# Batch 0 as one block of 512 columns and eight blocks behind it, batches 0 and 1 by a written list of steps, weights converted 1024 columns at a time

## The chip, the cores and the metric

The kernel runs on one core of a Trainium2 chip. The metric is the device time of one launch in microseconds (us). TensorE (PE, and PEld for its weight loads), VectorE (DVE), ScalarE (ACT), GpSimd (POOL) and SyncE (SP, which issues all the DMAs here) run their own instruction streams, each in order.

## The reference

Attention within chunks of 64 positions, then an MLP mixer over tokens and channels. There are 8 batches, 8 heads, 576 positions and 64 features per head; DT is 256 and DC is 1536.

```python
scores = scale * np.matmul(q_c, k_c.transpose(0, 1, 2, 4, 3))     # per chunk of 64
scores = scores - np.max(scores, axis=-1, keepdims=True)
attn = np.exp(scores); attn = attn / (np.sum(attn, axis=-1, keepdims=True) + 1e-09)
out = np.matmul(attn, v_c)                                         # x: [8, 576, 512]
h = np.maximum(xt @ w_tok1, 0.0) @ w_tok2                          # xt: x transposed
u = x + h.transpose(0, 2, 1)
return u + np.maximum(u @ w_ch1, 0.0) @ w_ch2                      # 512 -> 1536 -> 512
```

The four weights are 64-bit floats in memory, all else is 32-bit.

## The kernel before

**Columns.** The mixer works on u with features on partitions and (batch, position) pairs as columns: 8 x 576 = 4608 columns. Batch 0 is done first, as two halves of 288 columns (`HALF`). Then come the other 4032 columns as `BLOCKS`: six of 512 and two of 480. The first two (`SINGLE`) run one by one. The other six run as three pairs in `pair` and `pair_end`, by a scheme that forms seven products for the eight of two blocks (`ps_p`, from weight sums stored in DRAM and read back through a `ring`).

**One block.** For each of the twelve slices f of the 1536 hidden features, `ch1` forms 12 matmuls into `ps_c` (four groups of input features, and three terms, `THREE`, since each operand is split into a high and a low part), ScalarE takes the ReLU as `gh`, VectorE the remainder as `gl`, and `ch2` adds 12 matmuls into the four accumulators `acc`. So a block that isn't in a pair costs 288 matmuls of its width; a pair costs 252 for `ps_p` and 288 for `acc`.

**Batch 0.** The loop over f forms `ch1` for the first half, `ch1` for the second half, whose ReLU is parked in `g1` (`kept=True`), and `ch2` for the first half. A second loop then splits the parked values (`split_g`) and does `ch2` for the second half. The token mixing of batch 0 (`tok1_first`, `tok2`) runs in plain fp32; `tok2` adds x by transposing matmuls. The second half's `tok2` stands behind the first `ch1`.

**Weights.** `plan` lists 29 pieces: five of the token weights, and 24 of 512 columns in turn from w_ch1 (`c1`) and w_ch2 (`c2`). Each takes four steps on ScalarE (`wtop`, `low` and its second half in `words_clamp`, `kept` in `split_high`) and four on VectorE (clamp, shift, add, `split_low`). `conversion()` is a generator; `convert(n)` places its next n VectorE steps, by counts in tables (`FIRST_FILL`, `END_FILL`, `STEP_FILL`). The token weights are converted at the start, and their parts for later batches are split in the second loop of batch 0 (`SPLIT_AT`).

**Attention.** There are 36 tiles, nine for two batches; the fifth of the nine is shared by both. A tile is: scores (32 matmuls of 64 columns), row maximum, subtraction, exp, transposition, values (32 matmuls), division. The five tiles of batch 0 transpose on TensorE (`near`). Those of batch 1 (`part`, placed by `STARTS`) transpose in 32 x 32 blocks on VectorE and finish through DRAM: `far` is written, and read back as `pf`. Tiles of batches 2 to 7 run in "bursts" (`attention`, `LAG` 2: the values of a tile stand two bursts behind its scores). The first two bursts stand in the second loop of batch 0 (`FIRST_QK`), fourteen in the two single blocks (`BURSTS`, a place being one `ch1` or one `ch2`), the others in the pairs.

**What sets the order.** Up to the first `start_ps.close()` the source's order holds on TensorE, ScalarE and VectorE. Between there and `HAND_FROM` a list scheduler orders them; from there on TensorE is again in the source's order (`by_hand`), and `in_turn` holds single steps behind the last one. SP is in the source's order throughout.

Of the kernel before, what the change touches and what calls it, by code (L numbers as in the profile page):

```python
# [18 lines left out]
P = 128  # L19
# [10 lines left out]
HALF = S // 2  # L30
# [19 lines left out]
BURSTS = (2, 6, 9, 13, 17, 20, 23, 26, 30, 34, 37, 38, 40, 43)  # L50
# [3 lines left out]
TOKENS_AT = (19, 35, 44)  # L54
# [5 lines left out]
KEPT_AT = {18 + k: ((k // 3, (0, 1, 5)[k % 3]),) for k in range(18)}  # L60
# [7 lines left out]
AHEAD = 3  # L68
RUN = 4

WARM_T = (0, 1, 0, 0, 0)
WARM_V = (0, 0, 1, 0, 0)
FIRST_FILL = (2, 2, 2, 3, 1)
PREPARE = (0, 1, 2, 1, 1)

END_FILL = (3, 2, 2, 3, 6, 1, 1)
STEP_FILL = (2, 4, 4, 4, 4, 4, 4, 2, 0, 2, 5, 3, 0, 8, 5, 4, 4, 5, 7, 4, 1, 1, 5, 3)

STARTS = ((9, 10, 10, 10, 14), (13, 14, 15, 16, 16), (17, 18, 18, 19, 22), (23, 23, 24, 26, 27))
# [26 lines left out]
def attention_mixer_kernel(ctx, tc, qk_in, vo_in, v_in, w1_in, w2_in, wc1_in, wc2_in, out):  # L108
# [68 lines left out]
    fetched = []  # L177

    def fetch(n):
        for i in range(len(fetched), min(n, len(plan))):  # L180
            fetched.append(i)
            key, src, lo, n = plan[i]
            nc.sync.dma_start(
                out=raws[i][1].rearrange("p n w -> p (n w)"), in_=src[:, lo:lo + n].bitcast(I32)
            )

    def words_scalar(i):

        fetch(i + AHEAD)
        n = plan[i][3]
        st = raws[i][1]
        if i < token:
            if "t" not in tops:
                tops["t"] = pool.tile([P, sum(p[3] for p in plan[:token])], F32, tag="wtt", name="wtt", bufs=1)
            lo = sum(p[3] for p in plan[:i])  # L200
            tops[i] = tops["t"][:, lo:lo + n]
        else:
            tops[i] = pool.tile([P, n], F32, tag="wt", name="wtop", bufs=4)
        lows[i] = pool.tile([P, max(n, DM)], I32, tag="low" if n < S else "low_t", name="low", bufs=3)[:, :n]
        nc.scalar.activation(out=tops[i], in_=st[:, :, 1].bitcast(F32), func=AF.Copy, scale=REBIAS)  # L205
        nc.scalar.activation(  # L206
            out=lows[i].bitcast(I16)[:, 0::2], in_=st[:, :, 0].bitcast(U32), func=AF.Copy, scale=2.0 ** -29
# [3 lines left out]
    def words_clamp(i):  # L211
        nc.vector.tensor_scalar(
            out=tops[i], in0=tops[i], scalar1=-MOST, scalar2=MOST, op0=ALU.max, op1=ALU.min
        )
        nc.scalar.copy(out=lows[i].bitcast(F16)[:, 1::2], in_=tops[i])
# [43 lines left out]

    def split_high(i):  # L260
# [1094 lines left out]
```

## Time and profile before

| | us |
|---|---|
| median of three runs (lowest, highest) | 741.07 (738.27, 741.98) |
| the profiled execution, its own time | 743.39 |
| the profiled execution, its span | 741.4 |
| TensorE busy, 5730 matmuls | 717.3 |
| VectorE, ScalarE, GpSimd busy | 437.1, 275.4, 189.6 |

The span runs from the first instruction to the last one. Matmuls overlap, so busy time of TensorE is no measure of how close it comes to its rate; the number of matmuls in a stretch is. "Idle before" names what ended the wait of an engine.

### The profile page before, as it was taken

The numbers are of one execution on the slowest core, as the hardware profiler recorded it, in microseconds if no ns is written. First come the engines' busy times: TensorE is split into PE (matmuls) and PEld (weight loads), VectorE is DVE, ScalarE is ACT, GpSimd is POOL, SyncE is SP. The second block draws the span as 40 slices with busy tenths as digits, with TensorE's granted clock in tenths as the row PEclk, the third lists the DMA queues.
The fourth block names the chain that finished last, engine by engine and source line by source line (L and its number), as shares of the span: only waits on it lengthen the run. The fifth ranks groups of instructions, "written<-read, shape, count | busy, mean of one in ns | idle before, by whom it ended". The sixth has DMA issues, their size and how long they took to land.

```text
span 741.4 us, 14629 instructions
## 1 busy us (share of the span) xinstructions
PE 717.3 (97%) x5730; PEld 629.7 (85%) x5730; DVE 437.1 (59%) x735; ACT 275.4 (37%) x505; POOL 189.6 (26%) x161
## 2 busy tenths in 40 slices
PE   6899998999999999989999999999999999999997
PEld 4488898988889877878888888988888899999997
DVE  4799966555546546577666763686343539433361
ACT  5899953333332333332333333332211324112120
POOL 0000012162346543103111163061112602311220
PEclk8999999999999999999999999999999999999999
DMA  9956346669855676745888995045655430644111
GB/s 344 407 218 222 118 157 198 218 202 290 289 178 185 202 229 224 237 127 197 268 261 272 284 312 139 12 140 161 192 177 182 138 93 21 235 135 126 53 54 53
DMA packets 93268, 139.94 MB, mean 189 GB/s; under 512 B 10832, under 2 KB 44880, under 8 KB 93200
## 3 DMA queue, kind: packets, MB, share of 16 engines
q1 hardware_dynamic: 93200, 139.02, 57.0%
q8 instruction: 45, 0.74, 0.4%
q14 instruction: 23, 0.19, 0.1%
HBM read 98.34 MB, written 39.71 MB: 186 GB/s over the span
## 4 chain that ended last, share of the span: by engine, by line
PE 74%; DMA 8%; DVE 6%; ACT 5%; SPq 4%; issue 2%; POOL 0%; DVEq 0%; ACTq 0%; POOLq 0%
PE acc L1121 24%; PE ps_p L1051 21%; PE acc L726 8%; PE ps_c L682 7%; PE ps_t L653 5%; PE ps_t L581 4%; SPq L406 2%; DMA far<-blocks 2%; PE ps_sv L372 2%; PE ps_sv L384 1%; DMA raw_t<-in_w 1%; DVE wtop L225 1%; ACT low L206 1%; PE sum L590 1%; ACT wtop L205 1%
## 5 line engine op out<-in xcount | busy, mean ns | idle before, releaser
L1121 PE MATMUL acc<-gh,kept_c 128*128 128x512 f32 (+1 forms) x576 | 169.5, 376 | 0.0
L1051 PE MATMUL ps_p<-bh,ring 128*128 128x512 f32 (+1 forms) x504 | 148.5, 376 | 0.1
L1121 PEld LDWEIGHTS acc<-gh,kept_c 128*128 128x128 f32 x576 | 108.2, 189 | 12.8
L1121 PE MATMUL acc<-gl,kept_c 128*128 128x512 f32 (+1 forms) x288 | 107.9, 375 | 0.0
L1051 PEld LDWEIGHTS ps_p<-bh,ring 128*128 128x128 f32 x504 | 94.6, 189 | 11.8 <-DVE sum L1146 0.5
L1051 PE MATMUL ps_p<-bl,ring 128*128 128x512 f32 (+1 forms) x252 | 94.4, 375 | 0.0
L726 PE MATMUL acc<-gh,kept_c 128*128 128x288 f32 (+1 forms) x384 | 91.1, 341 | 1.7 <-ACT gh L695 1.5
L484 POOL TENSOR_TENSOR xl<-x,xh 128x512 fp32r<-128x512 f32 x28 | 37.7, 1358 | 160.4 <-ACT xh L483 137.2
L726 PEld LDWEIGHTS acc<-gh,kept_c 128*128 128x128 f32 x384 | 63.7, 192 | 8.2 <-ACT gh L695 2.8
L1148 POOL TENSOR_TENSOR sum<-snap,sum 128x512 f32<-128x512 f32 (+1 forms) x18 | 23.1, 1282 | 167.4 <-ACT snap L1140 144.7
L1121 PEld LDWEIGHTS acc<-gl,kept_c 128*128 128x128 f32 x288 | 54.4, 189 | 6.5
L682 PE MATMUL ps_c<-uh,kept_c 128*128 128x512 f32 x192 | 57.8, 383 | 1.3 <-DVE rl L600 1.3
L726 PE MATMUL acc<-gl,kept_c 128*128 128x288 f32 (+1 forms) x192 | 57.1, 336 | 0.0
L1051 PEld LDWEIGHTS ps_p<-bl,ring 128*128 128x128 f32 x252 | 47.6, 189 | 5.7
L1153 ACT ACTIVATE gh<-c 128x512 fp32r<-128x512 f32 (+1 forms) x36 | 22.4, 622 | 77.3 <-DVE c L1146 73.4
L352 ACT ACTIVATE pr<-pr 128x512 f32<-128x512 f32 x36 | 22.6, 628 | 76.6 <-DVE pr L348 76.6
L1140 ACT COPY snap<-ps_p 128x512 f32<-128x512 f32 (+1 forms) x36 | 20.8, 577 | 75.5 <-PE ps_p L1051 71.9
L1154 DVE SCALAR_TENSOR_TENSOR gl<-g,gh 128x512 fp32r<-128x512 f32 (+1 forms) x36 | 32.9, 936 | 24.4 <-ACT gh L1153 24.4
L696 DVE SCALAR_TENSOR_TENSOR gl<-ps_c,gh 128x512 fp32r<-128x512 f32 (+1 forms) x36 | 21.8, 605 | 40.1 <-ACT gh L695 40.0
L682 PE MATMUL ps_c<-both,kept_c 128*128 128x288 f32 x288 | 41.2, 291 | 1.0 <-DVE gl L696 1.0
L682 PEld LDWEIGHTS ps_c<-uh,kept_c 128*128 128x128 f32 x192 | 35.7, 189 | 6.8 <-DVE rl L600 1.7
L682 PEld LDWEIGHTS ps_c<-both,kept_c 128*128 128x128 f32 x288 | 37.2, 189 | 2.2 <-DVE gl L696 1.4
(134 smaller groups left out, 1257.8 us busy)
## 6 DMA issues: line engine op xcount, KB each, us to landing
ring<-w SPq DMA_DIRECT2D x126, 256.0 KB, 4.0
qk<-in_qk SPq DMA_DIRECT2D x36, 512.0 KB, 4.8
far<-blocks SPq DMA_DIRECT2D x63, 256.0 KB, 2.9
raw_c<-in_wc SPq DMA_DIRECT2D x24, 512.0 KB, 9.3
pf<-far SPq DMA_DIRECT2D x124, 64.0 KB, 2.4
v<-in_v SPq DMA_DIRECT2D x27, 256.0 KB, 4.6
xt<-far SPq DMA_DIRECT2D x96, 64.0 KB, 2.0
w<-sparts SPq DMA_DIRECT2D x24, 256.0 KB, 2.7
```

Of the source, the lines that this page charges most:

```text
L352: nc.scalar.activation(out=pr, in_=pr, func=AF.Exp, scale=1.0 / float(D) ** 0.5)
L484: nc.gpsimd.tensor_tensor(out=xl, in0=t["own"], in1=xh.bitcast(F32), op=ALU.subtract)
L581: nc.tensor.matmul(ps, lhsT=lhsT, rhs=in_turn_of_two(rhs), start=(n == 0 and q == 0), stop=(n == len(mt) - 1 and q == len(terms) - 1),)
L653: nc.tensor.matmul(ps[:, at:at + n], lhsT=lhsT[:, cols], rhs=rhs.rearrange("p (c a b) -> p c b a", a=2, b=RUN), start=(q == 0), stop=(q == ...
L682: nc.tensor.matmul(ps[:, :width], lhsT=weights["c1", f][:, wi, k // 2, k % 2 * P:(k % 2 + 1) * P], rhs=in_turn_of_two(u[ui][k]), start=(k ...
L696: nc.vector.scalar_tensor_tensor(out=halved(gl), in0=ps, scalar=0.0, in1=halved(gh.bitcast(F32)), op0=ALU.max, op1=ALU.subtract)
L726: nc.tensor.matmul(accs[e], lhsT=weights["c2", f][:, wi, e * P:(e + 1) * P], rhs=in_turn_of_two(g[gi]), start=(f == 0 and q == 0), stop=(f ...
L1051: nc.tensor.matmul(ps, lhsT=w[:, wi, j * P:(j + 1) * P].bitcast(F32R), rhs=in_turn_of_two(u[ui][j]), start=j == 0 and q == 0, stop=j == 1 ...
L1121: nc.tensor.matmul(accs[e], lhsT=weights["c2", f][:, wi, e * P:(e + 1) * P], rhs=in_turn_of_two(g[gi]), start=start and q == 0, stop=stop ...
L1148: engine.tensor_tensor(out=c, in0=a, in1=b, op=ALU.add)
L1153: nc.scalar.activation(out=gh, in_=c, func=AF.Relu)
L1154: nc.vector.scalar_tensor_tensor(out=gl, in0=c, scalar=0.0, in1=gh.bitcast(F32), op0=ALU.max, op1=ALU.subtract)
```

## The change

Batch 0 becomes one block of its first 512 columns; the 64 that are left (`REST`) go into the next block, beside 448 of batch 1, so that all eight `BLOCKS` are 512 wide. The parking in `g1`, `split_g` and the last blocks of 480 go away. `u` of a block is one tile for each part. Of the 64 columns, `more` does the token mixing, and `moreh`, `morel` put them into block 0.

`plan` has 15 pieces: two of w_tok1, one of w_tok2, and twelve of 1024 columns (two f each). Its steps are no longer placed by a generator: the string `ORDER` names every step of batches 0 and 1, from the first load to the end of batch 0's `ch2`, and TensorE, ScalarE, VectorE and SP all take it in that order. `F` fetches a piece, `top low clamp sign shift add high rest` are its eight steps; `s max sub exp` and `t` or `far`, then `pt v za zb o end split` those of an attention tile; `u uh ul` the token mixing of batch 0; `ca gh gl cb` a slice's `ch1`, its two parts and its `ch2`; `hidden rh rl turn` batch 1's token mixing; `D` stores weights. The shared fifth tile of batches 0 and 1 is stacked in `stack`. Of batch 1's tiles the last transposes on TensorE (`t8`). The parts of the token weights are split earlier (`high0`, `high1`, `high2`). All sixteen first bursts stand in the single blocks.

```diff
-HALF = S // 2
+REST = S - 512
-BLOCKS = [(k * N, N) for k in range(2 * PAIRS)]
-LAST = ((B - 1) * S - 2 * PAIRS * N) // 2
-BLOCKS += [(2 * PAIRS * N + k * LAST, LAST) for k in range(2)]
+BLOCKS = [((k + 1) * N, N) for k in range(SINGLE + 2 * PAIRS)]
-BURSTS = (2, 6, 9, 13, 17, 20, 23, 26, 30, 34, 37, 38, 40, 43)
+BURSTS = (0, 3, 6, 9, 12, 15, 18, 21, 24, 27, 30, 33, 36, 38, 40, 43)
-TOKENS_AT = (19, 35, 44)
+TOKENS_AT = (21, 36, 44)
...
+ORDER = """
+LQ0 F0 LV0 LQ1 LV1 LQ2 F1 LV2 LQ3 LV3 LQ4 LV4 F2 F3 F4 F5 F6 F7 LQ5 LV5 F8 LQ6 LV6 F9 F10 s0 max0 top0
+sub0 low0 clamp0 exp0 sign0 s1 t0 shift0 max1 pt0 add0 s2 sub1 high0 max2 exp1 v0 rest0 top1 t1 za0 sub2
...
+low6 ul1 s5 clamp6 uh3 max5 low7 ul3 sub5 ca0 sign6 rest4 exp5 end4 top7 shift6 ca1 far5 gh0 clamp7 high5
+F11 LQ7 LV7 gl0 sign7 add6 cb0 gh1 rest5 high6 shift7 stack0 ca2 gl1 top8 add7 low8 clamp8 ca3 rest6
...
+rest2 gh7 pt7 morel0 gl7 v7 add14 LV9 cb7 D5 za7 high14 zb7 o7 rest14 split7 s8 LQ10 gh9 end7 cb8 max8
+gl9 sub8 ca10 exp8 gh10 gl10 t8 pt8 cb9 v8 LV10 za8 zb8 o8 ca11 split8 end8 gh11 gl11
+hidden0 rh0 rl0 hidden1 rh1 rl1 cb10 turn0 cb11
+"""
...
-    plan = [(("t1", j, min(2, NKT - j)), w1_in, j * DT, min(2, NKT - j) * DT) for j in range(0, NKT, 2)]
-    plan += [(("t2", k), w2_in, k * S, S) for k in range(NT1)]
+    plan = [(("t1", 0, 2), w1_in, 0, 2 * DT), (("t1", 2, 3), w1_in, 2 * DT, 3 * DT)]
+    plan += [(("t2", 0, NT1), w2_in, 0, NT1 * S)]
     token = len(plan)
-    for f in range(-1, NFC):
-        plan += [(("c1", f + 1), wc1_in, (f + 1) * DM, DM)] if f < NFC - 1 else []
-        plan += [(("c2", f), wc2_in, f * DM, DM)] if f >= 0 else []
+    for f in range(0, NFC, 2):
+        plan += [(("c1", f, 2), wc1_in, f * DM, 2 * DM), (("c2", f, 2), wc2_in, f * DM, 2 * DM)]
...
+    def first_mix(ps, m, whole, at, stop):
+        cols = slice(m * P, (m + 1) * P)
+        for t, rows, j in mix_tiles(0):
+            if j * P in range(at, stop):
+                n, x = rows.stop, tiles[t].get("own", tiles[t]["x"])
+                nc.tensor.matmul(
+                    ps[:, j * P - at:j * P - at + n], lhsT=x[rows, cols], rhs=ident[rows, :n],
+                    start=(j * P == at), stop=False, is_transpose=(n == P),
+                )
         for k in range(NT1):
             nc.tensor.matmul(
-                ps, lhsT=r[k][:, cols], rhs=tops["t2", k][:, n * HALF:(n + 1) * HALF],
+                ps, lhsT=whole[k][:, cols], rhs=tops["t2", k][:, at:stop],
                 start=False, stop=(k == NT1 - 1),
             )
...
+    def first_u(m):
+        if "u" not in us:
+            us["u"] = block_u()
+        own[m] = ps_acc.tile([P, 512], F32, tag="acc", name="ps_t2")
+        first_mix(own[m], m, r, 0, N)
+    def channel_out(f):
+        ch2(0, N, us["u"], f, gs.pop(f), accs)
...
+    for step in ORDER.split():
+        kind = step.rstrip("0123456789")
+        steps[kind](int(step[len(kind):]))
+    start_ps.close()
+    by_hand.close()
```

Three places of the built programs show the moves. The first is TensorE where batch 0's channel products begin: `ps_s` are scores, `ps_c` channel products, the rows with `ident` and `r` are batch 0's token mixing, `both` and `uh` hold u. Before:

```order
L626 MATMUL ps_t_695<-wtt,r 128x288 x2
L329 MATMUL ps_s<-qk 64x64
L682 MATMUL ps_c_719<-both,kept_c_0_559 128x288 x2
L329 MATMUL ps_s<-qk 64x64 x4
L682 MATMUL ps_c_719<-both,kept_c_0_559 128x288 x3
L619 MATMUL ps_t_745<-ident,x 128x96
L619 MATMUL ps_t_745<-ident,x 128x128
L619 MATMUL ps_t_745<-ident,x 128x64
L626 MATMUL ps_t_745<-wtt,r 128x288 x2
```

And now:

```order
L606 MATMUL ps_t_570<-ident,x 128x128 x4
L611 MATMUL ps_t_570<-wtt,r 128x512 x2
L606 MATMUL ps_t_582<-ident,x 128x128 x4
L611 MATMUL ps_t_582<-wtt,r 128x512 x2
L295 MATMUL ps_s<-qk 64x64 x16
L660 MATMUL ps_c_628<-uh,kept_c_0_2_541 128x512 x2
L660 MATMUL ps_c_628<-ul,kept_c_0_2_541 128x512
```

The token mixing of 512 columns now stands whole ahead of the first channel product; before, that of the second half stood between products of the first.

The second is ScalarE at the same place: `wtop`, `low` and `kept` are steps of a piece of weights. Before:

```order
L205 ACTIVATE wtop<-raw_c_3_161 128x512
L206 ACTIVATE low<-raw_c_3_161 128x512
L215 CAST low<-wtop 128x512
L270 CAST kept_c_1_669<-wtop 128x512
L205 ACTIVATE wtop<-raw_c_2_157 128x512
L206 ACTIVATE low<-raw_c_2_157 128x512
L215 CAST low<-wtop 128x512
L630 CAST both<-ps_t_681 128x288
```

And now:

```order
L190 ACTIVATE wtop<-raw_c_2_2_125 128x1024
L772 ACTIVATE r<-sum 128x512
L239 CAST kept_c_0_2_541<-wtop 128x4x256
L196 ACTIVATE low<-raw_c_2_2_125 128x1024
L208 CAST low<-wtop 128x1024
L783 CAST uh<-ps_t_546 128x512
L208 CAST low<-wtop 128x1024
L783 CAST uh<-ps_t_559 128x512
L190 ACTIVATE wtop<-raw_c_2_2_121 128x1024
```

Half as many steps of twice the width stand between the other steps.

The third is VectorE at batch 1's last tile, whose scores feed `mx` and `pr`. Before:

```order
L345 TENSOR_REDUCE mx<-ps_s 128x8
L219 TENSOR_SCALAR wtop<-wtop 128x512
L278 TENSOR_TENSOR kept_c_11_1525<-wtop,kept_c_11_1525 128x2x256
L348 TENSOR_TENSOR pr<-ps_s,mx 128x2x4x64
L278 TENSOR_TENSOR kept_c_10_1559<-wtop,kept_c_10_1559 128x512
L225 ISA wtop<-wtop,low 128x1024
L696 SCALAR_TENSOR_TENSOR gl<-ps_c_1438,gh 128x288
L395 STREAM_TRANSPOSE blocks<-pr 128x4x4x32
```

And now:

```order
L310 TENSOR_REDUCE mx<-ps_s 128x8
L674 SCALAR_TENSOR_TENSOR gl<-ps_c_1208,gh 128x512
L315 TENSOR_TENSOR pr<-ps_s,mx 128x2x4x64
L674 SCALAR_TENSOR_TENSOR gl<-ps_c_1333,gh 128x512
L429 TENSOR_SCALAR zi<-ps_v 128x8
L432 RECIPROCAL zi<-zi 128x8
L439 TENSOR_TENSOR x<-ps_v,zi 128x512
L370 STREAM_TRANSPOSE blocks<-x 128x4x4x32
L674 SCALAR_TENSOR_TENSOR gl<-ps_c_1394,gh 128x512
L584 SCALAR_TENSOR_TENSOR rl<-ps_t_1423,rh 128x512
```

The transposition of `pr` on the way to DRAM is gone from this tile; the last steps of the weights stand ahead of it, and only `gl` steps between.

## Rows read from the trace of the kernel before

**Rows 1.** The page: busy time, share of the span, matmuls of TensorE.
```profile
PE 717.3 (97%) x5730; PEld 629.7 (85%) x5730; DVE 437.1 (59%) x735; ACT 275.4 (37%) x505; POOL 189.6 (26%) x161
```
**Rows 2.** Windows: busy us (instructions) of PE, PEld, DVE, ACT, POOL; granted clock, DMA.
```profile
0.00:42.30 42.30, 32.52 (x409) 20.27 (x409) 27.81 (x63) 30.59 (x52) 0.92 (x10) 0.88 0.98 380
42.30:149.40 107.10, 102.02 (x983) 94.32 (x982) 81.30 (x164) 72.36 (x143) 13.14 (x12) 0.98 0.53 176
149.40:337.50 188.10, 182.71 (x1708) 159.35 (x1701) 108.27 (x181) 64.66 (x118) 74.06 (x65) 0.99 0.67 213
337.50:741.40 403.90, 400.03 (x2642) 355.78 (x2640) 219.71 (x331) 107.83 (x193) 101.51 (x75) 1.00 0.50 161
```
**Rows 3.** Source lines: matmul count, duration ns, first and last start in us.
```profile
L682 PE MATMUL ps_c<-both,kept_c x288: 286/286/500, 42.3 to 110.5; 128*128 128x288 f32 x144
L682 PE MATMUL ps_c<-uh,kept_c x192: 379/379/483, 149.4 to 332.1; 128*128 128x512 f32 x192
...
L1051 PE MATMUL ps_p<-bh,ring x504: 366/379/484, 337.7 to 704.2; 128*128 128x512 f32 x112, 128*128 128x480 f32 x56
```
**Rows 4.** Windows, TensorE alone (matmuls): widths 288, 512 and 480; granted clock.
```profile
98.85:101.79 2.94, 2.94 (x24) 1.00 0.22 83
...
550.00:600.00 50.00, 50.00 (x233) 1.00 0.49 165
650.00:700.00 50.00, 50.00 (x249) 1.00 0.38 116
```
**Rows 5.** Chain of waits, 42 to 150 us: start, us, what.
```profile
115.02 4.71 DMA far<-blocks
121.11 1.96 DMA pf<-far
123.22 0.63 ACT pt L423
```
**Rows 6.** Windows, TensorE alone, behind the wait for that tile: granted clock third last.
```profile
124.40:127.80 3.40, 3.40 (x28) 0.50 1.05 381
```
**Rows 7.** Waits of TensorE, 42.3 to 149.4 us: total, times, longest.
```profile
PE ps_v L442 <- ACT pt L423: 2.3, 2, 2.0
```
**Rows 8.** Timeline of TensorE at the start: start, us, what.
```profile
28.46 1.98 PE L590 MATMUL sum<-x,wtt 128*128 128x512 f32 x4
...
36.19 0.58 PE L619 MATMUL ps_t<-ident,x 128*128 128x128 f32 x4
36.61 1.22 PE L626 MATMUL ps_t<-wtt,r 128*128 128x288 f32 x4
...
46.10 0.83 PE L619 MATMUL ps_t<-ident,x 128*128 128x96 f32 x5
...
47.72 0.74 PE L682 MATMUL ps_c<-both,kept_c 128*128 128x288 f32 x3
```
**Rows 9.** Timeline of TensorE: one tile's scores and the matmul behind them.
```profile
111.09 0.69 PE L329 MATMUL ps_s<-qk 64*64 64x64 f32 x32
111.72 0.51 PE L726 MATMUL acc<-gh,kept_c 128*128 128x288 f32 x2
```
**Rows 10.** Groups of ScalarE: count, busy us, mean ns; the first to 115 us, others from 149.4.
```profile
L206 ACT ACTIVATE low<-raw_c 128x512 int16<-128x512 uint32 x24 | 18.8, 784 | 0.0
...
L695 ACT ACTIVATE gh<-ps_c 128x512 fp32r<-128x512 f32 x24 | 14.3, 595 | 25.7 <-PE ps_c L682 25.4
...
L1023 ACT CAST sparts<-sparts 128x1024 fp32r<-128x1024 f32 x6 | 6.2, 1040 | 6.8 <-POOL sparts L1017 6.8
```
**Rows 11.** Timeline of ScalarE: two weight steps in a row, and the last weight step.
```profile
22.42 0.76 ACT L206 ACTIVATE low<-raw_c 128x512 int16<-128x512 uint32 x1
23.05 0.67 ACT L205 ACTIVATE wtop<-raw_c 128x512 f32<-128x512 f32 x1
...
99.37 0.62 ACT L270 CAST kept_c<-wtop 128x512 fp32r<-128x512 f32 x1 [0.33 <-DVE wtop L225]
```
**Rows 12.** The page: DMA issues, KB each, median us to landing.
```profile
raw_c<-in_wc SPq DMA_DIRECT2D x24, 512.0 KB, 9.3
```

More of the change, by code (lines that the diff above doesn't have):

```diff
@@ L710, in ch2 @@
     def ch2(at, width, u, f, g, accs):
-        while ("c2", f) not in weights:
-            convert(1)
-        whole = at + width == B * S
         if f == 0:
             accs[:] = [ps_acc.tile([P, 512], F32, tag="acc", name="acc")[:, :width] for _ in range(NDT)]
-        if f == NFC - 2 and whole:
-            for e in range(NDT):
-                o = pool.tile([P, N], F32, tag="o", name="o", bufs=8)[:, :width]
-                nc.gpsimd.tensor_tensor(
-                    out=o, in0=u[0][e].bitcast(F32), in1=u[1][e].bitcast(F32), op=ALU.add
-                )
-                accs.append(o)
@@ L864, in attention_mixer_kernel @@
-    last_of = {}
-    extra = {}
-    for slot, job, *of in JOBS:
-        extra.setdefault(slot, []).append((job, of))
-    def extras(slot):
-        for job, of in extra.get(slot, ()):
-            {"ready": ready, "part": part, "split": split}[job](*of)
+    first, second = batch_tiles(0), batch_tiles(1)
+    order = [t for b in range(2, B) for t in sorted(batch_tiles(b), key=lambda t: t % NTILE != 4)]
+    queue = (*first, *second, *order)
     wide = ctx.enter_context(tc.tile_pool(name="wide", bufs=1, space=bass.MemoryType.DRAM))
@@ L901, in attention_mixer_kernel @@
[L901 to L917 removed]
+    sums = [ps_sum.tile([P, 512], F32, tag="sum", name="sum") for _ in range(NT1)]
@@ new lines, in attention_mixer_kernel, with stack, stack_high, stack_low @@
+    r = [pool.tile([P, DM], F32, tag="gr", name="r", bufs=12) for _ in range(NT1)]
+    us, own, psums, gs, accs = {}, {}, {}, {}, []
+    rs = {1: [[None, None] for _ in range(NT1)]}
+    def stack(k):
+        if k == 0:
+            attn_stack(first[4], range(1, 2))
+            return
+        (stack_high if k == 1 else stack_low)()
+    def stack_high():
+        tiles[first[4]]["rest"][0]()
+    def stack_low():
+        tiles[first[4]].pop("rest")[1]()
+    def relu(k):
+        if k == 0:
+            nc.scalar.activation(out=r[0], in_=sums[0], func=AF.Relu)
+        else:
+            nc.vector.tensor_scalar_max(out=r[1], in0=sums[1], scalar1=0.0)
@@ new lines, in scores, with values, end @@
+    def scores(i):
+        attn_s(i, *(ps_first, "first") if i < NKT else ())
+    def values(i):
+        attn_v(i, *(ps_first, "first") if i < NKT else ())
+    def end(i):
+        if i == first[4]:
+            tiles[i]["own"] = tiles[i]["x"]
+            tiles[i]["x"] = far_out(tiles[i]["x"], "far_x")
+            close_tile(i)
+        else:
+            attn_end(i)
+        load_waiting(9)
+    steps = {
+        "F": fetch, "LQ": lambda j: load_qk(queue[j]), "LV": lambda j: load_v(queue[j]), "D": dump_kept,
+        "top": words_top, "low": words_low, "clamp": words_clamp, "sign": words_sign, "shift": words_shift,
+        "add": words_add, "high": split_high, "rest": split_low, "half": half,
+        "s": scores, "max": attn_max, "sub": attn_sub, "exp": attn_exp, "t": attn_near, "pt": attn_t,
+        "v": values, "za": attn_sum, "zb": attn_inverse, "o": attn_o, "far": attn_far, "end": end,
+        "split": attn_split, "stack": stack, "tok": lambda j: tok1_first(j, sums), "relu": relu,
+        "u": first_u, "uh": first_high, "ul": first_low, "more": more, "moreh": more_high, "morel": more_low,
+        "ca": channel_sum, "gh": channel_high, "gl": channel_low, "cb": channel_out,
+        "hidden": token_sum, "rh": token_high, "rl": token_low, "turn": lambda k: turn(k, rs, us[k]),
+        "warm": warm,
+    }
```

532 lines of the change are left out of this document (203 added, 329 removed).

## The prediction

> **What bounds the kernel now.** I read the page first. TensorE is busy 97% of the span, the other engines 59% or less [rows 1], so the time is TensorE's work plus what it loses; busy time hides the loss, because matmuls overlap. The table by stage comes next [rows 2], its edges taken from the first starts of three kinds of matmul [rows 3]: the first channel product of batch 0 at 42.3 us, that of the next block at 149.4, the first product of the pairs at 337.5 (the row gives its first recorded start, 337.7). The rates come from clean stretches [rows 4]: 24 matmuls of 288 columns in 2.94 us, 0.1225 us each; 233 of 512 in 50 us, 0.2146; 249 of 480 in 50 us, 0.2008. These are 0.425, 0.419 and 0.418 ns a column: width as such buys little, and the gain must come from fewer columns or less loss.
>
> The stage from 42.3 to 149.4 holds 107.1 us. Its work: 576 matmuls of 288, 70.6; the second half's token mixing, 4 x 1.62 (46.10 to 47.72) = 6.5 [rows 8]; eight groups of scores or values of batch 1's four tiles and the scores of two bursts, ten at 0.63 (111.09 to 111.72) = 6.3 [rows 9]; batch 1's first token product, 28 x 0.2146 = 6.0; its second, 24 x 0.2146 = 5.2. That is 94.6, so 12.5 us are lost. Late in the stage the chain of waits shows why [rows 5]: the last tile of batch 1 goes through DRAM (4.71 and 1.96 us), TensorE waits 2.0 us for the copy of it [rows 7], and behind that wait the granted clock is 0.50, the lower level of 1.2 GHz, for 3.4 us, in which 28 matmuls start [rows 6]; at half rate that stretch loses 1.7. Earlier in the stage the chain lies on weight steps: ScalarE is busy 72.4 of 107.1 us [rows 2], but its weight steps end only at 99.4 [rows 11].
>
> A rule speaks on the rates. The Trainium skill ("TensorE: Matmul & The Clock Gate", section "Back-to-back issue gap") gives about 131 ns for each matmul of 512 in a sustained stream. The rows here show 214.6 ns, so the trace disagrees; by the page the 288 matmuls of the new batch 0 would take 37.7 us in place of the 61.8 below, and the sum would be 24 us lower. I go by the row.
>
> **The change part by part.**
>
> *Where batch 0's products begin.* The new order puts the whole token mixing of 512 columns ahead of them. Before, it began at 36.2 [rows 8]. One group is four transposes, 0.42 us (36.19 to 36.61), and two fp32 products of 512 columns, 1.98 (the row of four records at 28.46). Four groups make 9.6, so the products begin at 36.2 + 9.6 = 45.8. A check from ScalarE, which must have done four and a half pieces of 1024 and all the token pieces by then: about 43 steps' worth of 512 columns at 0.6 us (0.63 from one weight step to the next, [rows 11]), 26; fifteen other steps of 0.6, 9; and the 11.7 us in which it was idle up to there before (42.3 less 30.6 busy, [rows 2]): 46.7. From both sides: 43, if the tiles finish earlier because fewer weight steps stand before them in ScalarE's list, and 50, if pieces twice as wide hold the first product up.
>
> *TensorE's work from there to the next block.* 288 x 0.2146 = 61.8; three scores and four values at 0.63, 4.4; the last tile's transposes, 0.4; the 64 columns left over, 4 groups of about 0.3 from [rows 8] (0.42 + 1.98 for 512 columns, by width), 1.2; batch 1's token products, 6.0 and 24 x 448 columns, 4.5. Sum 78.3.
>
> *Loss.* The last tile no longer goes to DRAM, so its 2.0 us wait and the slow 1.7 behind it go: 12.5 falls to 8.8. What is late next there is the token product behind it: after its values stand a `ca` of 2.6 us and most of the token product before its rows are needed, 8.6 us in all, and it needs a division, ScalarE's copy (0.6) and GpSimd's remainder: covered. The parked half's extra steps go as well (12 ReLUs and 12 copies on ScalarE, as many on VectorE). I take 7, with 3 and 12.5 as the ends. So the next block begins at 45.8 + 78.3 + 7 = 131.1, 18.3 us earlier.
>
> *Weights 1024 at a time.* Where the trace has both widths, the wide ScalarE cast is 1040 ns, the narrow ones 595 to 784 [rows 10]; 96 steps become 48 on each engine. For two f ScalarE now needs eight such steps at 1.04 to 1.26 (twice 0.63), two `gh` at 0.6 and two tile steps' share of 1.3: 10.8 to 12.6. TensorE needs 48 x 0.2146 + 0.8 = 11.1. They are level, and ScalarE is ahead when the products begin (five pieces of twelve begun), so I price this at nothing beyond the loss above; TensorE is the cover, and if it goes, each 1 us that a pair of f takes longer costs up to 6 us.
>
> *Moved DMAs.* Pieces 11 to 14 now stand in SP's list behind writes to DRAM and reads of them that wait for VectorE. Piece 11 stands some twenty ScalarE steps ahead of its first use, about 20 us, against 9.3 from issue to landing for half its size [rows 12]: 2 us of that slack may go, nothing more. The weight stores `D` keep their number. GpSimd's remainders of batch 1's tiles stay in the stage.
>
> *Single blocks.* Two bursts' scores move in here: 2 x 0.63 = +1.3. Sixteen bursts in the same 48 places also bring 14% more VectorE steps and DMAs of that kind; VectorE is busy 108 of 188 us [rows 2], so I add nothing, with +4 as the end if their waits reach TensorE. Below nothing there is no reason.
>
> *Third pair.* 252 + 288 matmuls go from 480 to 512 columns: 540 x (0.2146 - 0.2008) = +7.5. TensorE is busy 400 of the pairs' 403.9 us [rows 2], so nothing hides it.
>
> *Sum.* -18.3 + 1.3 + 7.5 = -9.5. The profiled execution took 743.4 with its span of 741.4, so it would be 733.9; the median of the runs is 2.3 lower, 741.07, so 731.5.
>
> **The rivals.**
>
> *Loss stays* (12.5: other waits replace the DRAM one). For it: the three engines' lists are now locked together, and TensorE, ScalarE need 11.1 and 10.8 to 12.6 us for two f. Against it: the longest wait named in that stage is gone. The block begins at 136.6: -12.8 + 8.8 = -4.0, 737.1.
>
> *Wide pieces come late.* The first product needs a piece of 1024 columns through all eight steps, and the others are as coarse: products begin at 50 and 12.5 is lost. 140.8: -8.6 + 8.8 = +0.2, 741.3. The Trainium skill ("Perfetto Trace Analysis", section "Optimizing Scalar/DVE Operations") states this: where ScalarE and VectorE aren't saturated but cause bubbles on other engines, breaking instructions up may finish work sooner. By that rule the widening is wrong here; no run so far shows it.
>
> *Starved and slowed* (slower). If weights arrive behind TensorE at every pair of f, TensorE waits and its granted clock falls to 1.2 GHz behind the wait, as behind the 2.0 us wait of [rows 7]: 2.0 + 1.7 a time, six times, 22 us for the 7. The block begins at 146.1: -3.3 + 8.8 = +5.5, 746.6. It decides once ScalarE or VectorE needs over 13 us for two f (11.1 + 2.0); the rows give 12.6 at most, which speaks against it. VectorE sharing its time with more tile steps speaks for it.
>
> *The 64 columns and the 512 bring nothing by themselves*: batch 0's products shrink by 70.6 - 61.8 = 8.8 and the third pair grows by 7.5. That is part of every case above: without a smaller loss there is little gain.
>
> **How the numbers follow.** Forecast 45%; loss stays 22%; wide pieces late 17%; starved 10%; better than forecast (products at 43, loss 3: 124.3, so -25.1 + 8.8, 724.8) 6%. The bounds for 8 in 10: below, that best case with nothing added to the single blocks, 724; above, the late case with half of the +4, 743. A measurement here can tell about 0.5%, 3.7 us, so faster means under 737.4 and slower over 744.8. Faster: most of the forecast, the better case, half of "loss stays", a little of the late case: 0.64. Slower: the starved case and a share of the late one: 0.13. Same: 0.23.
>
> **What would show it.** The first `ps_c` of batch 0 near 46 us, the first of the next block near 131, the third pair 7.5 us longer, and no wait of TensorE on a copy of the last tile. A first start after 50, `ps_c` or `acc` waiting on `gh` or `gl` for 1 us and more several times, or stretches at clock 0.5 past 50 us would make it wrong. So would new waits of TensorE in the single blocks, which I priced at nothing.

## The result, and the profile after

The changed kernel takes 747.1 us (median of six runs, 745.1 to 749.9), the kernel before 741.0 in six runs beside it: a ratio of 1.0095, 95% interval 1.0065 to 1.0124. It is about 1% slower. The forecast was 731.5, with a range of 724 to 743: wrong in sign and outside the range. The profiled execution took 746.25 us with a span of 744.4; against the one before (743.39) that is 2.9 more. The medians differ by 6.15, since the profiled execution before was 2.4 above its median and this one 0.9 below its own.

The page's busy line and the table of stages after, to hold against [rows 1] and [rows 2]; columns as there:

```profile
PE 713.5 (96%) x5432; PEld 608.6 (82%) x5432; DVE 430.0 (58%) x659; ACT 269.6 (36%) x422; POOL 189.3 (25%) x157
```
```profile
0.00:41.80 41.80, 32.83 (x437) 19.32 (x437) 30.29 (x54) 32.88 (x40) 0.91 (x10) 0.96 0.97 387
41.80:133.25 91.45, 86.43 (x596) 71.82 (x593) 63.97 (x90) 62.51 (x71) 9.86 (x7) 0.98 0.53 179
133.25:332.00 198.75, 185.55 (x1765) 159.95 (x1764) 110.63 (x187) 65.70 (x120) 75.72 (x65) 0.97 0.66 209
332.00:744.40 412.40, 408.73 (x2641) 357.49 (x2640) 225.11 (x331) 108.49 (x193) 102.82 (x75) 1.00 0.49 158
```

The next block's products begin at 133.25 in place of 149.4, 16.15 us earlier, nearly what was forecast (131.1). The single blocks take 198.75 in place of 188.1, 10.65 longer, where the forecast had 1.3. The pairs take 412.4 in place of 403.9, 8.5 longer, forecast 7.5. -16.15 + 10.65 + 8.5 = +3.0, the difference of the spans, where the forecast had -9.5. So the failure lies in the single blocks. In that stage TensorE is busy 185.6 us of 198.75, 13.2 less than the stage (5.4 less before), and its waits are these (total, times, longest):

```profile
PE ps_t L563 <- DVE gl L674: 7.1, 1, 7.1
PE ps_sv L359 <- ACT pt L399: 5.3, 1, 5.3
PE ps_t L563 <- POOL xl L461: 0.8, 1, 0.8
```

Two waits make nearly all of it. The first in TensorE's timeline: the scores of a burst, then nothing until the copy `pt` of the tile two bursts back is there. And ScalarE's timeline around it:

```profile
159.59 0.69 PE L347 MATMUL ps_sv<-qk 64*64 64x64 f32 x32
165.59 1.13 PE L359 MATMUL ps_sv<-v,pt 64*64 64x64 f32 x32 [5.30 <-ACT pt L399]
```
```profile
155.44 0.21 ACT L336 ACTIVATE zs<-zs 128x8 f32<-128x8 f32 x1
163.65 0.61 ACT L487 CAST xr<-xc 64x512 fp32r<-64x512 f32 x1 [8.01 <-DMA xc<-x]
164.29 0.60 ACT L669 ACTIVATE gh<-ps_c 128x512 fp32r<-128x512 f32 x1
164.91 0.62 ACT L399 COPY pt<-pf 128x512 f32<-128x512 f32 x1
```

ScalarE does nothing for 8.0 us: the next step in its list is `xr<-xc`, half of the stacking of a shared tile, whose rows come by a DMA. The ReLU `gh` and the copy `pt`, which TensorE needs, stand behind it. The second wait, at 264, looks different in TensorE's row (a token product behind VectorE's `gl`) and is the same on ScalarE, with an idle time of 9.9 us:

```profile
257.93 0.21 ACT L336 ACTIVATE zs<-zs 128x8 f32<-128x8 f32 x1
268.00 1.26 ACT L487 CAST xr<-xc 64x512 fp32r<-64x512 f32 x2 [9.87 <-DMA xc<-x]
269.17 1.04 ACT L960 CAST sparts<-sparts 128x1024 fp32r<-128x1024 f32 x1
270.11 0.61 ACT L399 COPY pt<-pf 128x512 f32<-128x512 f32 x1
270.63 0.59 ACT L669 ACTIVATE gh<-ps_c 128x512 fp32r<-128x512 f32 x1
```

Here `gh` stands behind `xr`; until `gh` and `gl` have read their channel product, its PSUM buffer isn't free, and the second token product needs it. Nothing in TensorE's own row names the step that is to blame; it is found two engines further up. Behind both waits the granted clock is down to about its lower level, 1.2 GHz (windows of TensorE, granted clock third last):

```profile
165.60:169.00 3.40, 3.40 (x38) 0.53 0.99 299
...
272.00:274.50 2.50, 2.50 (x6) 0.50 0.71 224
```

Why `xc` comes so late is in SP's timeline, here between the first bursts; the tile it comes from is divided by VectorE at 153.35:

```profile
151.33 0.38 SPq L375 DMA_DIRECT2D far<-blocks  x1
151.75 2.72 SPq L381 DMA_DIRECT2D xt<-far  x4
155.78 1.73 SPq L381 DMA_DIRECT2D pf<-far  x4
...
158.97 1.13 SPq L479 DMA_DIRECT2D xc<-x  x2
```

`xc` is issued at 158.97, 5 us after its data exist: SP, in order, is still at the burst before, whose four reads `pf` wait for `far` to land (issued at 151.33, 4.4 us). ScalarE's step on it begins 4.7 us after that. SP's waits for `far` in this stage, before and after, and ScalarE's for `xc`, before and after:

```profile
SPq L406 <- DMA far<-blocks: 15.7, 8, 4.2
...
ACT xr L510 <- DMA xc<-x: 4.9, 2, 3.2
```
```profile
SPq L381 <- DMA far<-blocks: 24.6, 12, 5.2
...
ACT xr L487 <- DMA xc<-x: 17.9, 2, 9.9
```

The same step waited before as well, 3.2 us at most, and no wait of TensorE stands behind it there.

### The profile page after: what moved, and what is told of

Same layout as the page of the kernel before. It is cut to its first block, busy times and chain, and to the rows that moved or that the text cites. A ratio compares the mean times of both kernels' runs of the same rounds, so it can differ in the third digit from the quotient of the medians.

```text
span 744.4 us, 13807 instructions
## 1 busy us (share of the span) xinstructions
PE 713.5 (96%) x5432; PEld 608.6 (82%) x5432; DVE 430.0 (58%) x659; ACT 269.6 (36%) x422; POOL 189.3 (25%) x157
## 4 chain that ended last, share of the span: by engine, by line
PE 74%; DMA 10%; ACT 6%; SPq 5%; DVE 3%; issue 2%; POOL 0%; ACTq 0%; DVEq 0%
PE acc L1055 25%; PE ps_p L988 22%; PE ps_t L631 6%; PE acc L693 6%; PE ps_t L563 5%; PE ps_c L660 5%; DMA far<-blocks 4%; SPq L381 4%; DMA raw_t<-in_w 2%; PE ps_sv L347 2%; PE ps_sv L359 1%; ACT wtop L190 1%; DMA v<-in_v 1%; ACT low L196 1%; ACT low L208 1%
## 5 line engine op out<-in xcount | busy, mean ns | idle before, releaser
L1055 PE MATMUL acc<-gh,kept_c 128*128 128x512 f32 x576 | 172.0, 380 | 0.0
L988 PE MATMUL ps_p<-bh,ring 128*128 128x512 f32 x504 | 150.6, 380 | 0.0
L1055 PE MATMUL acc<-gl,kept_c 128*128 128x512 f32 x288 | 109.2, 379 | 0.0
L988 PE MATMUL ps_p<-bl,ring 128*128 128x512 f32 x252 | 95.5, 379 | 0.0
L693 PE MATMUL acc<-gh,kept_c 128*128 128x512 f32 x288 | 88.3, 388 | 1.0 <-ACT gh L669 1.0
L660 PE MATMUL ps_c<-uh,kept_c 128*128 128x512 f32 x288 | 88.2, 388 | 0.0
L1082 POOL TENSOR_TENSOR sum<-snap,sum 128x512 f32<-128x512 f32 x18 | 23.3, 1294 | 170.9 <-ACT snap L1074 133.0
L693 PE MATMUL acc<-gl,kept_c 128*128 128x512 f32 x144 | 55.5, 385 | 0.8 <-DVE gl L674 0.6
L660 PE MATMUL ps_c<-ul,kept_c 128*128 128x512 f32 x144 | 54.8, 381 | 0.0
L1088 DVE SCALAR_TENSOR_TENSOR gl<-g,gh 128x512 fp32r<-128x512 f32 x36 | 35.4, 1013 | 18.6 <-ACT gh L1087 13.8
L674 DVE SCALAR_TENSOR_TENSOR gl<-ps_c,gh 128x512 fp32r<-128x512 f32 x36 | 24.5, 680 | 33.6 <-ACT gh L669 29.7
L1088 DVE SCALAR_TENSOR_TENSOR gl<-c,gh 128x512 fp32r<-128x512 f32 x36 | 25.7, 714 | 22.0 <-ACT gh L1087 21.9
```

The costliest lines, as they stand in the source:

```text
L660: nc.tensor.matmul(ps, lhsT=weights["c1", f][:, wi, k // 2, k % 2 * P:(k % 2 + 1) * P], rhs=in_turn_of_two(u[ui][:, k]), start=(k == 0 and ...
L674: nc.vector.scalar_tensor_tensor(out=halved(gl), in0=in_order(ps), scalar=0.0, in1=halved(gh.bitcast(F32)), op0=ALU.max, op1=ALU.subtract)
L693: nc.tensor.matmul(accs[e], lhsT=weights["c2", f][:, wi, e * P:(e + 1) * P], rhs=in_turn_of_two(g[gi]), start=(f == 0 and q == 0), stop=(f ...
L988: nc.tensor.matmul(ps, lhsT=w[:, wi, j * P:(j + 1) * P].bitcast(F32R), rhs=in_turn_of_two(u[ui][j]), start=j == 0 and q == 0, stop=j == 1 ...
L1055: nc.tensor.matmul(accs[e], lhsT=weights["c2", f][:, wi, e * P:(e + 1) * P], rhs=in_turn_of_two(g[gi]), start=start and q == 0, stop=stop ...
L1082: engine.tensor_tensor(out=c, in0=a, in1=b, op=ALU.add)
```

## Experiments

Theory A: a step of ScalarE that nobody needs soon holds back those that TensorE waits for. Theory B, later D: SP's queue makes everything late. Theory C: bursts three places apart are too dense as such. Times are medians, with the ratio to the kernel before and its 95% interval. The kernel before read 738.75 to 741.0 beside them, so two experiments are best compared by their ratios. A stage is read from one profiled execution, and kernels with the same first stage show it between 88.9 and 91.8 us; so differences of 2 us in a stage tell nothing.

**The step later.**

```diff
-                stack_end(j)
+                if k > LAG:
+                    stack_end(order[k - LAG - 1])
```

> One change to the kernel after: the second half of a shared tile's stacking (ScalarE's xr<-xc and VectorE's remainder behind it) is placed one burst later, 9 us; its DMA stays where it is. Theory A (ScalarE's list: it waits 8.0 and 9.9 us for xc, and the ReLU and the copy that TensorE needs are queued behind that): TensorE's waits of 5.3 us at 160 and 7.1 us at 264 both go, ScalarE waits under 2 us for xc between 133 and 332 in place of 17.9, the single blocks shrink from 198.6 to 183-187 us, and the time from 747.1 to 731-735. Theory B (SP's queue and the DMAs are late with everything, pf too): waits of the same size stay on pt<-pf, time 743-748.

Measured: 742.8 us, 1.0033 [1.0004, 1.0063]; single blocks 196.6. The wait at 160 is gone and `xc` is no longer among ScalarE's waits, yet TensorE still waits 5.9 us at 263, and waits of 2.3 us at 178 (for `pt`) and 2.8 us at 200 (for `xl`) are new or longer. ScalarE's row there, and the chain of waits that leads to it (start, us, what):

```profile
266.01 1.04 ACT L961 CAST sparts<-sparts 128x1024 fp32r<-128x1024 f32 x1 [9.73 <-DMA qk<-in_qk]
```
```profile
259.03 3.90 DMA w<-sparts
...
263.09 2.09 POOL sparts L955 x3
```

The row's releaser, `qk`, isn't the one: the step reads GpSimd's sums, and these waited for SP to store the sums before them out of the only buffer (`w<-sparts`, issued behind eight reads of `xt`). So a second step stood right behind the first, late for as long. Taking one away gained, by the ratios, about a third of what A said, and in the stage itself 2.2 us of the 12 to 16. A was incomplete, B wrong on the first wait.

**Fewer DMAs ahead of the first shared tile; a place more behind each shared tile.**

```diff
-        load_waiting(1)
+        quiet = k in (1, 2)
+        load_waiting(0 if quiet else 1)
...
-TOKENS_TO = (3, 7, 10, 14, 18, 21)
+TOKENS_TO = (9, 10, 11, 14, 18, 21)
```

> The kernel after with SP's queue relieved ahead of the first shared tile only: bursts 1 and 2 issue no reads of xt (made up by later bursts), and two weight stores of that stretch come later; ScalarE's list is untouched. Theory A with a late queue as the reason why xc is late: some 8 reads and 2 stores of 0.43-0.47 us leave the front of SP's queue, xc lands 3-4 us earlier, TensorE's wait at 160 falls from 5.3 to 1-2 us, that at 264 stays 7 us, time 741-744. If SP's queue has no part in it, the wait at 160 stays over 4 us and the time 745-748.

Measured: 753.1, 1.0162 [1.0116, 1.0209]; single blocks 206.7. The wait at 160 fell to 2.7 us, but one of 4.1 us for `xl` at 206 and this one near 271 grew:

```profile
PE ps_t L563 <- DVE gl L674: 8.9, 1, 8.9
```

The first wait moved as forecast, the time (741 to 744) was missed by 9 us. That the reads put off only came later in the same queue is the likely reason; no run tests it alone.

```diff
-BURSTS = (0, 3, 6, 9, 12, 15, 18, 21, 24, 27, 30, 33, 36, 38, 40, 43)
+BURSTS = (0, 3, 6, 10, 12, 15, 18, 21, 24, 27, 30, 33, 37, 39, 41, 43)
```

> The kernel after with the burst behind each shared tile's values one place later (9 to 10, 36 to 37, with 38 to 39 and 40 to 41), all else as it is. Theory A: at 160 the copy pt gets 3 us more, so that TensorE's wait falls from 5.3 to 2-3 us; at 264 the victim is the token product, whose PSUM buffer is held by a ReLU queued behind xr, and its place is the same, so about 7 us stay; time 743-746. Theory C (the bursts 3 places apart are too dense as such): both waits fall by the same, time 735-741.

Measured: 743.1, 1.0036 [1.0012, 1.0060]. At 160 the wait is 2.4 us, as A said; at 200 and 270 there are 4.1 and 4.6 us, on `xl` and `rl`, where A had 7 at 264. The time is at A's lower end and above C's range, and the rows are A's: ScalarE waits even longer for `xc`, 20.5 us in all.

**A move in the first stage on top** (a part of one line of `ORDER`).

```diff
-rest2 gh7 pt7 morel0 gl7 v7 add14 LV9 cb7 D5 za7
+rest2 gh7 morel0 gl7 add14 LV9 cb7 D5 pt7 v7 za7
```

> The kernel of e1_stack_later with one more move, in the first stage: the copy and the values of batch 1's tile 7 stand behind the ch2 of f=7 in place of ahead of it, 2.6 us later. Theory A: the wait of 2.5 us at 97 (pt<-pf) goes, and what the granted clock lost behind it; the next block begins at 129-131 in place of 133.3; time 2-4 us below e1_stack_later, 728-732. Rival: the wait only moves to the next tile or to the token product behind it, and the time equals that of e1_stack_later within 1 us.

Measured: 742.3, 1.0033 [1.0005, 1.0062], the same as e1; first stage 90.05 against 89.85. The rival held: the tile's values only run later.

**SP's queue made shorter.**

```diff
-            far_in(t.pop("far"), t["pf"])
+            nc.sync.dma_start(out=t["pf"].rearrange("p a b c -> p (a b c)"), in_=t.pop("far"))
```

> The kernel after with each burst's four reads pf<-far made one read of the same 256 KB, in straight order: what is left out is the transposition of the attention weights of batches 2 to 7, so their values are of other numbers; every engine's work is the same. Theory D, which the four runs before leave: SP issues one DMA after another and waits for each far to land, and a burst every three places is more than it can carry (some 229 issues of about 0.5 us and 25 us of waiting for far in 199 us), so whatever ScalarE takes from it comes late: xr, pt and the weight sums, whose buffer is free only once SP has stored it. 3 x 16 issues fewer, 0.47 us each, leave the single blocks: the waits at 160 and 264 shrink from 5.5 and 7.2 to under 3 us each, the blocks to 186-191 us, the time to 735-740. Theory A alone (ScalarE's list, with DMA time as it is): xc still lands 2-5 us late, waits stay over 4 us, time 743-747.

Measured: 738.8, 1.0010 [0.9983, 1.0037]; single blocks 190.7. The waits are 2.7 and 4.3 us. As D said in time, less so in the second wait (under 3 forecast). One read in place of four also changes how the data lie, so it isn't the number of issues alone.

```diff
-            nc.sync.dma_start(out=stored[key], in_=src if src.dtype == F32 else src.bitcast(F32))
+            (nc.sync if src.dtype != F32 else nc.gpsimd).dma_start(out=stored[key], in_=src if src.dtype == F32 else src.bitcast(F32))
```

> The kernel after with the 24 stores of weight sums (w<-sparts) issued by GpSimd in place of SP, correct and all else as it is. Theory D: 24 issues and their place in the queue leave SP, GpSimd's next sums no longer wait for a store behind reads of xt; the wait at 264 falls from 7.2 to 3-5 us (xc is still late), that at 160 stays 4-5.5, time 742-745. If SP's queue has no part in it: both waits and the time stay (745-748).

Measured: 746.2, 1.0096 [1.0066, 1.0126]; single blocks 200.3. No gain: D was wrong here, which had 742 to 745 and a wait of 3 to 5 us at 264. It is 8.2, and that at 160 is 6.4, for `xr` is still the step that holds ScalarE at 267:

```profile
267.84 1.25 ACT L487 CAST xr<-xc 64x512 fp32r<-64x512 f32 x2 [10.96 <-DMA xc<-x]
```

**Both together** (the edits of e1 and e6).

> e6_sums_on_pool_queue and e1_stack_later together: the two steps that held ScalarE at 264 in turn (xr in the kernel after, the split of the weight sums in e1) are both taken out of the way. Theory D: the wait at 264, 6.0 us in e1, falls under 2 us; what is left are the waits at 177 and 200 for pt (2.5 and 2.9 us in e1), smaller by 1 us each; time 734-738. Theory A alone: the same as e1, 741-744.

Measured: 734.25, 0.9925 [0.9896, 0.9953], 0.75% faster than before. The single blocks, then what TensorE waits for from 41 us on:

```profile
133.61:319.20 185.59, 181.98 (x1766) 157.27 (x1765) 112.01 (x187) 65.75 (x120) 89.39 (x89) 1.00 0.70 224
```
```profile
PE ps_v L418 <- ACT pt L399: 3.5, 2, 2.7
PE ps_t L563 <- DVE gl L674: 1.5, 1, 1.5
PE ps_sv L359 <- ACT pt L399: 1.4, 2, 1.0
```

The stage reads 198.75 with neither edit, 196.6 and 200.3 with one, 185.6 with both, and the four kernels built on both show 184.4 to 189.3. At 264 this is what two holds on one list look like: the later one decides, and each edit alone seems worthless. At 160 the first edit works alone, but the late sums then make other waits: in e1 they stand ahead of the copy `pt` on ScalarE at 178 and of `xl` on GpSimd at 200. GpSimd's wait until its sums are stored, in e1 and in e7:

```profile
POOL sparts L955 <- DMA w<-sparts: 35.3, 4, 11.9
...
POOL sparts L955 <- DMA w<-sparts: 4.9, 2, 4.3
```

SP's queue is as late as ever (its waits for `far` are 37.4 us here, 24.6 in the kernel after); what changed is that little of what TensorE needs stands behind it.

The same two edits in the kernel before, as a control:

> The kernel before with the same two moves as e7_sums_and_stack (stacking of a shared tile one burst later; weight sums stored through GpSimd). Theory A+D (ScalarE is held only where the bursts of the kernel after stand three places apart and xc and the sums come late): before, ScalarE waits 4.9 us for xc and 6.8 for sums and TensorE loses none of it by a named wait, so the time stays within 2 us, 737-741, and e7's gain is a repair of what the change broke. Rival (the two moves help any such kernel): 733-736.

Measured: 737.3, 0.9965 [0.9938, 0.9991]; single blocks 184.2 in place of 188.1. A gain of a third of a per cent, not the full one. So e7's gain is mostly a repair. But the holds weren't free before, as the expectation has it. Two of TensorE's waits in the single blocks of the kernel before, then ScalarE's row ahead of the second:

```profile
PE ps_t L653 <- DVE u L660: 3.1, 1, 3.1
PE ps_c L682 <- DVE rl L600: 1.3, 1, 1.3
```
```profile
271.39 1.04 ACT L1023 CAST sparts<-sparts 128x1024 fp32r<-128x1024 f32 x1 [4.22 <-POOL sparts L1017]
```

`rl` needs `rh`, which stands behind that late step on the sums; VectorE, which makes `u`, had waited 4.0 us for a late read of `xt` a little earlier. Both waits are gone in the control. Against this control the changed kernel with the repair is 0.4% lower, with intervals that overlap.

**The first stage: who bounds it?** On e7, one of ScalarE's steps on the weights goes to GpSimd:

```diff
-        nc.scalar.copy(out=lows[i].bitcast(F16)[:, 1::2], in_=tops[i])
+        out = lows[i].bitcast(F16)[:, 1::2]
+        if i >= token:
+            nc.gpsimd.tensor_copy(out=out, in_=tops[i])
+        else:
+            nc.scalar.copy(out=out, in_=tops[i])
```

> e7_sums_and_stack with one more move, in the first stage: one of ScalarE's four steps of each piece of w_ch1 and w_ch2 (the second half of low, 128x1024 cast, 1.21 us from start to start) goes to GpSimd, which is idle there. Theory: ScalarE, busy without a gap from 42 to 80 us, is what TensorE waits for in the first stage: it sheds 12 x 1.21 = 14.5 us, the next block begins at 125-129 in place of 133, and the time is 4-8 us under e7. Rival: the chain of one piece gets longer by GpSimd's slower copy (some 2.7 us by twice its 128x512 step of 1.4), the products start later or wait, and the time equals e7 within 2 us or is above it.

Measured: 735.45, 0.9951 [0.9933, 0.9969]; first stage 93.2 against 91.8. The rival held: ScalarE had 9.4 us less to do there and nothing came of it. From 41 to 100 us, a group of ScalarE and one of VectorE (count, busy us, mean ns, idle before) in e7, then the same in e8:

```profile
L239 ACT CAST kept_c<-wtop 128x1024 fp32r<-128x1024 f32 x9 | 9.6, 1062 | 3.4 <-DVE wtop L218 3.4
...
L246 DVE TENSOR_TENSOR kept_c<-wtop,kept_c 128x1024 fp32r<-128x1024 f32 x10 | 12.2, 1221 | 1.5 <-ACT kept_c L239 1.4
```
```profile
L243 ACT CAST kept_c<-wtop 128x1024 fp32r<-128x1024 f32 x10 | 10.4, 1043 | 10.1 <-DVE wtop L222 10.1
...
L250 DVE TENSOR_TENSOR kept_c<-wtop,kept_c 128x1024 fp32r<-128x1024 f32 x10 | 13.9, 1392 | 1.6 <-ACT kept_c L243 1.6
```

ScalarE now waits 10.1 us in place of 3.4 for VectorE's step ahead of it in a piece. And VectorE got slower beside GpSimd's new work: its steps with two inputs took 14% (`kept_c`) and 7% longer (the addition, 1219 to 1301 ns), one step with a single input not (691, 684), the other 12% (the shift, 686 to 766). The Trainium skill ("GPSIMD Engine Reference", section "1. Specifications") says that the two engines contend for SBUF where VectorE's instruction has two SBUF inputs; the two-input steps here agree, and the shift shows that not they alone are slowed.

Each weight step made as two of 512 columns, back to back, on e7:

```diff
+    def two(i, blocks=False):
+        if i < token:
+            return [slice(None)]
+        return [slice(0, 2), slice(2, 4)] if blocks else [slice(0, DM), slice(DM, 2 * DM)]
...
-        nc.scalar.copy(out=lows[i].bitcast(F16)[:, 1::2], in_=tops[i])
+        for s in two(i):
+            nc.scalar.copy(out=lows[i][:, s].bitcast(F16)[:, 1::2], in_=tops[i][:, s])
...
```

> e7_sums_and_stack with every step of a 1024-column piece of w_ch1 and w_ch2 on ScalarE and VectorE made as two instructions of 512, back to back, loads and order as they are. From start to start the traces show a piece's four ScalarE steps at 4.99 us wide (kernel after) against 2 x 2.38 = 4.77 narrow (kernel before), VectorE's at 3.51 against 2 x 1.88 = 3.75. Theory (width of an instruction is worth nothing; ScalarE is full from 42 to 80 either way): time within 1.5 us of e7, 733-736, first stage 91-93 us. Rival (the wide steps are what makes the first stage lose 13 us): first stage under 89 us, time under 732.

Measured: 737.7, 0.9954 [0.9930, 0.9979], which overlaps e7; first stage 91.3. Width decides nothing in the first stage, as expected. The time is above its forecast of 733 to 736, by the ratios 2 us above e7, and that isn't in the first stage.

**The last tiles of batch 1.** Tile 7 over TensorE too, and tile 8 back through DRAM, each on e7 (parts of lines of `ORDER`):

```diff
-exp7 gl6 gh8 far7 sign13 cb6 gl8
+exp7 gl6 gh8 sign13 cb6 t7 pt7 gl8
...
-gh7 pt7 morel0
+gh7 morel0
```

> e7_sums_and_stack with tile 7 of batch 1 transposed on TensorE, as tile 8 is, in place of going through DRAM. In e7 TensorE waits 2.7 us for its copy at 98, and the clock falls behind it. Theory (the wait for the last tile that goes to DRAM only moved from tile 8 to tile 7): the wait goes, with 1.7 us of low clock, for 0.4 us of transposes; the next block begins at 129-131 in place of 133.6; time 3-4 us under e7, 729-732. Rival (ScalarE or VectorE holds the stage): another wait takes its place, time within 1 us of e7.

Measured: 732.5, 0.9887 [0.9854, 0.9920], the fastest kernel here, 1.1% under the one before. The wait of 2.7 us is gone, the first stage takes 89.3. By the ratios it is 0.4% or 2.8 us under e7, just short of the forecast, and the intervals overlap; against the control e9 it is 0.8% lower, and these don't.

```diff
-exp8 gh10 gl10 t8 pt8 cb9 v8 LV10
+exp8 far8 gh10 gl10 cb9 LV10 pt8 v8
```

> e7_sums_and_stack with batch 1's last tile sent through DRAM again, as in the kernel before. The prediction priced its way over TensorE at a gain of 2.0 + 1.7 us less 0.4. By that: TensorE waits 2 us and more for its copy near 115, the clock behind it is at 0.5 for 3 us, the next block begins at 136-138, time 737-740. Rival (another wait is last there, as tile 7's is at 98): within 1 us of e7.

Measured: 737.45, 0.9957 [0.9935, 0.9980]; first stage 96.1, 4.3 longer than e7's. TensorE waits for the tile's copy, and the granted clock in the 3 us behind it is 0.67:

```profile
117.04 0.70 PE L418 MATMUL ps_v<-v,pt 64*64 64x65 f32 x32 [3.39 <-ACT pt L399]
```

## Why the prediction was wrong, point by point

**Single blocks: the step that failed.** I priced two more bursts at their scores, +1.3, and their waits at nothing "as VectorE is busy 108 of 188 us", with +4 as the end. Measured +10.65. Busy shares of VectorE and ScalarE (65.7 of 198.75 us even now) say nothing about an in-order list that stands still: ScalarE lost 17.9 us on one step. ScalarE's waits in that stage had no place in my sum: 4.9 us for `xc` and 6.8 for the sums were there before, at a cost to TensorE of 1.3 us (the wait of `rl` above), and the change moved the bursts from three or four places apart to three and with them what depends on `far`. SP I counted as a queue only for the weight pieces; its own waits for `far` in this stage, 15.7 us before and 24.6 after, weren't in the sum. With both holds removed the single blocks take 185.6 against 184.2 in the control. That fits the +1.3 for the work, though single executions, which differ by more, can't measure it; the waits, and the lower clock behind them, account for the error.

**Where batch 0's products begin.** 45.8 forecast, with 43 and 50 as ends; measured 41.8, below the lower end. I let the token mixing begin where it began before, at 36.2. It begins at 31.1 now and takes 10.0 us, near the 9.6:

```profile
31.14 0.66 PE L606 MATMUL ps_t<-ident,x 128*128 128x128 f32 x4
```

Fewer weight steps stand ahead of the tiles now; that this is the reason wasn't tested.

**Loss in the first stage.** Forecast 7, with 12.5 as the upper end. Measured 91.45 - 78.3 = 13.1. Some 2.5 of it are a term of the 78.3 that was too small: the 64 columns left over, which I took by width at 1.2 us, fill TensorE from 88.49 to 92.17, 3.7 us. Two of their rows (the first and the last):

```profile
88.49 0.43 PE L606 MATMUL ps_more<-ident,x 64*128 64x64 f32 x2
...
91.71 0.66 PE L611 MATMUL ps_more<-wtt,r 128*128 128x64 f32 x4
```

The errors of the beginning and of the loss nearly cancel (-4.0 and +6.1): that the next block came within 2.1 us of the forecast is luck, and "loss stays" was the better case. Some of the loss is the wait that I said would go: it moved from tile 8 to tile 7, 2.5 us at 97, and I named the token product as next in line and not the tile before. The price of the tile's way was about right: 2.0 + 1.7 - 0.4 = 3.3 against 4.3 in e11, where single executions of this stage differ by up to 3.

**Weights 1024 at a time.** Priced at nothing, and e12 agrees. From start to start, as 0.63 was read, the traces show a wide piece's four ScalarE steps at 4.99 us, 1.25 each: the upper end of the 1.04 to 1.26, whose lower end came from a plain cast. The steps themselves are longer, since each begins before the one ahead of it has ended. ScalarE's groups from 41.8 to 100 us after (mean ns), and from 42.3 to 115 us before:

```profile
L196 ACT ACTIVATE low<-raw_c 128x1024 int16<-128x1024 uint32 x9 | 14.4, 1602 | 0.0
L208 ACT CAST low<-wtop 128x1024 f16<-128x1024 f32 x9 | 12.6, 1416 | 0.1
L190 ACT ACTIVATE wtop<-raw_c 128x1024 f32<-128x1024 f32 x8 | 12.2, 1522 | 0.0
L239 ACT CAST kept_c<-wtop 128x1024 fp32r<-128x1024 f32 x9 | 9.8, 1093 | 3.2 <-DVE wtop L218 3.2
```
```profile
L206 ACT ACTIVATE low<-raw_c 128x512 int16<-128x512 uint32 x18 | 14.2, 788 | 0.0
L215 ACT CAST low<-wtop 128x512 f16<-128x512 f32 x18 | 13.6, 762 | 0.0
L205 ACT ACTIVATE wtop<-raw_c 128x512 f32<-128x512 f32 x18 | 12.2, 679 | 0.0
L270 ACT CAST kept_c<-wtop 128x512 fp32r<-128x512 f32 x11 | 6.8, 615 | 0.7 <-DVE wtop L225 0.7
```

By these mean durations a piece of 1024 takes 5.63 us wide and 2 x 2.84 narrow; from start to start it is 4.99 against 2 x 2.38. ScalarE saves nothing. The Trainium skill ("Perfetto Trace Analysis", section "Optimizing Scalar/DVE Operations") says that larger operations can improve the throughput of a saturated engine; ScalarE is saturated here from 42 to 80 us, and its rows don't show it (VectorE's steps gain a little, 3.51 against 3.75 us a piece). The other rule of that section of the Trainium skill, cited in the prediction against the widening, is for engines that aren't saturated, so e12, which breaks the steps up and finishes no sooner, doesn't test it.

**Third pair.** +7.5 forecast, +8.5 measured. The 540 matmuls were priced by width; I left out that the pair's token mixing gets wider too, which at the same rate is about 0.6 (an estimate: 24 matmuls of 64 more columns).

**Slower than before: the rival I had.** It was put into the first stage, as TensorE waiting at each pair of f. That didn't happen. A wait, and the lower clock behind it, is what happened, but in another place and for another reason; that its 746.6 lies so near the 747.1 is luck.

What stays open: how much of SP's lateness is the number of its issues and how much the slower landing of `far` (median 3.6 us after, 2.9 before), and what bounds the first stage. There ScalarE, VectorE and the round trips to DRAM are all close, and relieving one (e8) only shows the next. Undoing the spacing of the bursts alone, by putting two of them back into the first stage, wasn't tried; e7 shows that the spacing can stay and the time come back.

## What to carry to other kernels

Before packing more steps into a stage, list for each in-order engine the steps that wait for a DMA, and what stands behind each: an engine that is a third busy can still hold up the one that bounds the kernel. Put a step that nobody needs soon far behind its input, not right behind it. And where an edit that removes a named wait gains little, look at what that engine waits for next before giving up the theory: two holds in a row hide each other, and only both edits together show the price.

## What the runs showed of the hardware

ScalarE's steps on the raw 64-bit words took at least twice as long at twice the width (1602 against 788 ns, 1522 against 679), so nothing was saved by making them wider; the plain cast took less than twice (1093 against 615). Beside GpSimd's casts of 128 x 1024, 1.65 us each on average, VectorE's steps with two inputs took 7% and 14% longer, and one of two steps with a single input 12%. The 24 short matmuls of `ps_more` held TensorE for 3.7 us; by width I had priced them at 1.2.
